# Windowed attention with a gated MLP on one core: a small value matmul placed later, and the hand-written opening closed off behind its last steps

## The chip, the cores and the metric

One core of a Trainium2 chip runs the whole program. The metric is device microseconds of one execution; the kernel before has three timed runs, and every comparison is made with their median. A profile is one more execution, recorded by the hardware profiler. TensorE is called PE here, its weight loads PEld; VectorE is DVE, ScalarE is ACT, GpSimd is POOL, and SyncE (SP) issues the DMAs.

## The reference

Eight batches of eight heads, 576 positions, head size 64. Each query sees itself and the 127 positions before it, with a bias that falls with distance. The heads, put side by side, are the rows x of a gated MLP whose gate mixes positions.

```python
scores = scale * q @ k.T                       # per batch and head, 576 x 576
scores = where((rel >= 0) & (rel < 128), scores - slope[h] * abs(rel), -1e9)
attn = exp(scores - max);  attn /= attn.sum() + 1e-9
x = concat_heads(attn @ v)                     # 8 x 576 x 512
h = gelu_tanh(x @ w_in);  u, v = split(h)      # 512 and 512 columns
v_n = (v - mean) / sqrt(var + 1e-6) * g_ln
v_s = w_sg @ v_n + b_sg                        # over positions
out = x + (u * v_s) @ w_out
```

## The kernel before

**The attention** goes by pairs of heads: 32 pairs, four to a batch, pair n belonging to batch n // 4. A pair is a row of one-letter steps (the table STEPS). `a` and `c` are the score matmuls (`*` is both in one burst: `a` into the two banks of the PSUM pool ps_a, `c` into the two of ps_s); `A`, `C` and `n` run on DVE and form bias, row minima and their copy nb; `E` is the exponentials on ACT (line 373), `R` the reciprocal of the sums on DVE, `r`, `s` and `S` the scaling on POOL (line 388). `t` and `T` are four PE transposes each (line 398) for the first and the second head, `X` and `Y` DVE's masked copies of them out of ps_a (px). The first 64 queries have a narrower window and go apart: `z` is one transpose for them (line 411), `P` ACT's copy of it into p0 (line 414), and `2` or `3` the value matmul of these queries, p0 against vd (line 418, with 64 columns; the profile counts two passes of it), into ps_a or into ps_s. `V` (or `v`, in ps_a) is the value matmul of all other queries (line 431, 36 short ones), `x` gathers both results into SBUF on ACT (lines 439 and 440), and `h`, `l`, `k` split the pair's rows into a high and a low part (lines 446, 451, 455) in one of four buffers xs. A buffer of xs comes free when all that a batch's MLP reads of it is done.

**The MLP** of a batch is a generator, `mlp_block`, which yields after each chunk of matmuls the columns that it streamed: `t` (the last 64 positions, line 532), the two v parts (two chunks each of 12 matmuls with 512 columns, lines 501 to 503), four u parts (two chunks each of 12 matmuls with 288 columns, lines 478 to 480), four mixing parts g (two chunks of 14, lines 570 to 574) and four output parts. Each v, u, g and output part takes one of the two buffers of the PSUM pool ps_m. A v part's buffer is given back by ACT's gelu into vg (line 523), and vg has one buffer only: the second v part's gelu follows the first one's normalization (DVE line 486 to 490, POOL's power at line 489, ACT line 491, DVE line 494). A u part's buffer is given back by ACT's copy at line 550.

**The order.** For PE everything is fixed by the order in which the program is written: each PE instruction is chained to the one before (`in_order`). For the other engines the first stretch is fixed, the list START at lines 604 to 611: each token is a step and a pair (`e3`), a stage of splitting a weight (`d`, `m`, `b`, `o`, `+`, `H`, `-`), a load (`i`), or one quarter of a v part of batch 0 (`w12`). It holds pairs 0 to 4 and the split of w_in, and its instructions are chained on each engine. After START the table PLAN at line 654 says at which share of a pair's time in MLP columns its steps are put between chunks; a step lands behind the chunk in which its time falls. There DVE, ACT, POOL and SP have no written order: the framework's scheduler orders them at build time, by its own clock, and may place instructions that are written later ahead of START's remaining ones on these engines. The splitting of w_sg and w_out (`decode`) is handed out along the DVE steps of the later pairs.

The order of PE around the steps of this change, in the batch with pairs 21 to 24 (chunks in small letters, a and b being the halves), was

```
*22  v2b  t21 z21  v0a  T21 3_21  v0b  V21  u0a u0b u1a  *23  u1b u2a  t22 z22  u2b
T22 3_22  u3a u3b g0a  V22  g0b g1a  *24  g1b g2a  t23 z23  g2b  T23 3_23  g3a g3b  V23
```

Of the kernel before, what the change touches and what calls it, by code (L numbers as in the profile page):

```python
# [21 lines left out]
def attention_gmlp(  # L22
# [17 lines left out]
    nc = tc.nc  # L40
# [464 lines left out]
    def mlp_block(b, xs, xfs):  # L505
# [85 lines left out]
    FIRST = 5  # L591
# [15 lines left out]
        z1 C2 s1 q4 S1 t1 X1 a3 P1 f2 o5 T1 +5 Y1 h0 R2 d4 21 v1 A3 s2 l0 x1 L3 H5 t2 m4 k0 w10 b4 e3 X2 -5 w20  # L607
        c3 o4 w00 r2 C3 +4 z2 w30 P2 h1 S2 f3 a4 l1 T2 Y2 w31 H4 R3 k1 22 v2 -4 d3 A4 w01 r3 L4 x2 s3 w11 h2 m3
        t3 S3 e4 z3 X3 w21 l2 c4 T3 b3 w02 o3 k2 w32 Y3 P3 +3 d6 w12 C4 23 v3 H3 i7 -3 w22 x3 m6 h3 b6 f4 l3 o6
        w13 k3 +6 R4 w23 d7 w03 r4 H6 w33 m7 s4 z4 P4 b7 t4 S4 X4 -6 T4 o7 Y4 +7 24 v4 H7 -7 x4 h4 l4 k4  # L610
    """
    started = {}
    last = {}
    wchunks = {}

    @contextmanager
    def in_order(engines=None):

        before = len(nc.cur_bb.bb.instructions)
        yield  # L620
        for i in nc.cur_bb.bb.instructions[before:]:
            if engines is None or i.engine in engines:
                if i.engine in last:
                    tc.add_manual_dep(i, last[i.engine], mybir.DependencyInfo(mybir.DependencyClass.NoSync, mybir.DependencyReason.DATA), reason="in_order")
                last[i.engine] = i.name
# [22 lines left out]
    FULL = (4 * 3 * NC * F + 2 * NC * F + 6 * NC * S2 * NF + 2 * (3 * T + 2) * S2 * NF + 6 * NF * S2 * NC) / NPAIR  # L648
    BEGINS = [0, 0.95, 1.7, 2.4, 3.0, 3.6, 4.4]

    def begin(n):
        return BEGINS[n - FIRST] * FULL if n - FIRST < len(BEGINS) else (BEGINS[-1] + n - FIRST - len(BEGINS) + 1) * FULL

    PLAN = [(0.0, "*ACnq"), (0.45, "ER"), (0.8, "rsS"), (1.25, "tzXP"), (1.4, "TY3"), (1.7, "VxhlkL")]
    events = []
    for n in range(FIRST, len(pairs)):
        for at, ops in PLAN:
            k = n + int(at)
            t = begin(k) + (at - int(at)) * (begin(k + 1) - begin(k))
            events.append((t, ops, n))  # L660
    events.sort(key=lambda x: x[0])

    nc.sync.dma_start(gb, g_ln.rearrange("(o f) -> o f", o=1).broadcast_to([P, F]))
    vec.steps = steps = decode()
    now = 0
    PE = [nc.tensor.engine]
    for n in (FIRST, FIRST + 1):
        Pair.STEPS["q"](pairs[n])
        if n == FIRST:
            Pair.STEPS["L"](pairs[n])  # L670
    with in_order(PE):
        while True:
# [14 lines left out]
                break  # L687
            now += cols
    assert not events


# [23 lines left out]
```

## Time and profile before

| | |
|---|---|
| timed runs, us | 717.34, 717.72 (median), 718.35 |
| the profiled execution, us | 715.63, with a span of 713.9 from its first to its last instruction |
| granted TensorE clock, mean | 0.958 of full speed |
| DMA | 56.28 MB in the kernel's own queue, 25.2% of 16 engines' span |

The profiled execution is 0.3% under the median of the timed runs. A row of the timeline gives start, duration (both in us from the span's start), engine, line, operation, result and operands, and in brackets the idle time of the engine ahead of it with what ended that. A row of the chain of waits gives the waiting engine and what it waited for: the total in us, the number of times, and the longest. A row of the table by windows gives, for a stretch of the span, its length, each engine's busy time, the granted clock (1.00 is full speed), the DMA share and GB/s.

### The profile page before, as it was taken

What the parts mean: (1) busy time and instruction counts of PE and PEld (TensorE: products, weight loads), DVE (VectorE), ACT (ScalarE), POOL (GpSimd) and SP (SyncE); (2) the same over time, 40 slices, a digit from 0 to 9 for tenths busy, and PEclk for the clock granted to TensorE, in tenths of its full rate; (3) what the DMA queues carried; (4) which work ended last, traced back from release to release, by engine and by line L of the source; (5) the groups of instructions that cost most, each with busy time, mean ns of one, the idle gap of its engine ahead of it and who ended that gap; (6) DMA issues with size and microseconds to landing.
All of it is one profiled execution on the core that took longest, in us unless ns stands there. A gap on an engine that the chain in (4) does not pass through costs nothing.

```text
span 713.9 us, 14846 instructions
## 1 busy us (share of the span) xinstructions
PE 625.7 (88%) x5664; PEld 563.9 (79%) x5664; DVE 416.8 (58%) x1372; ACT 357.1 (50%) x997; POOL 246.6 (35%) x243
## 2 busy tenths in 40 slices
PE   3795678789889979999799997999799997999997
PEld 2574667677789958898589976899589985899997
DVE  5885848666755567555666547555665555643512
ACT  7775367424664265534656346543655337530430
POOL 1687345532335203441224403351124412331220
PEclk9998899899999998999899999999999998999999
DMA  8646321134212422223122331224122220101001
GB/s 272 212 122 203 99 76 53 36 119 119 69 41 65 136 67 69 61 68 115 34 69 68 102 102 36 62 62 136 50 68 70 86 86 2 34 1 67 1 1 67
DMA packets 55931, 57.24 MB, mean 80 GB/s; under 512 B 8498, under 2 KB 45362, under 8 KB 55860
## 3 DMA queue, kind: packets, MB, share of 16 engines
q1 hardware_dynamic: 55860, 56.28, 25.2%
q8 instruction: 45, 0.74, 0.4%
q14 instruction: 26, 0.21, 0.1%
HBM read 46.83 MB, written 9.44 MB: 79 GB/s over the span
## 4 chain that ended last, share of the span: by engine, by line
PE 47%; DVE 22%; ACT 20%; POOL 4%; issue 4%; DMA 2%; SPq 1%; POOLq 0%; ACTq 0%; DVEq 0%
ACT e L373 10%; PE ps_m L478 7%; PE ps_m L479 6%; PE ps_m L480 6%; DVE e L266 6%; PE ps_s L431 5%; PE ps_m L570 3%; PE ps_m L571 3%; PE ps_m L572 3%; DVE st L486 2%; DVE vn L494 2%; ACT L373 2%; ACT L523 2%; PE ps_a L330 2%; POOL rs L489 2%
## 5 line engine op out<-in xcount | busy, mean ns | idle before, releaser
L373 ACT ACTIVATE e<-e,nb 128x128 f32<-128x128 f32 x270 | 101.9, 379 | 75.9 <-DVE nb L266 75.7
L388 POOL TENSOR_TENSOR e<-e,rr 128x512 f32<-128x512 f32 (+1 forms) x96 | 80.1, 857 | 140.3 <-DVE rr L266 71.3
L489 POOL TENSOR_TENSOR rs<-rs,mhalf 128x1 f32<-128x1 f32 (+1 forms) x40 | 35.9, 909 | 171.7 <-DVE rs L488 171.7
L570 PE MATMUL ps_m<-ws,vn 128*128 128x288 f32 x256 | 79.8, 312 | 0.0
L478 PE MATMUL ps_m<-xs,wi 128*128 128x288 f32 x256 | 78.1, 305 | 0.0
L478 PE MATMUL ps_m<-g,wo 128*128 128x288 f32 x256 | 78.0, 305 | 0.0
L479 PE MATMUL ps_m<-g,wo 128*128 128x288 f32 x256 | 76.2, 298 | 1.1 <-POOL g L257 1.1
L571 PE MATMUL ps_m<-ws,vn 128*128 128x288 f32 x256 | 76.8, 300 | 0.0
L572 PE MATMUL ps_m<-ws,vn 128*128 128x288 f32 x256 | 76.8, 300 | 0.0
L480 PE MATMUL ps_m<-g,wo 128*128 128x288 f32 x256 | 76.0, 297 | 0.0
L479 PE MATMUL ps_m<-xs,wi 128*128 128x288 f32 x256 | 75.7, 296 | 0.0
L480 PE MATMUL ps_m<-xs,wi 128*128 128x288 f32 x256 | 75.6, 295 | 0.0
L257 POOL TENSOR_TENSOR g<-u,g 128x576 fp32r<-128x576 f32 x32 | 45.5, 1422 | 78.9 <-ACT g L256 78.9
L501 PE MATMUL ps_m<-wi,xs 128*128 128x512 f32 x128 | 58.1, 454 | 3.8 <-ACT xs L446 3.8
L266 DVE TENSOR_TENSOR px<-ps_a,m_old 128x512 f32<-128x512 f32 x64 | 43.7, 682 | 27.5 <-PE ps_a L398 27.2
L503 PE MATMUL ps_m<-wi,xs 128*128 128x512 f32 x128 | 54.8, 428 | 1.3 <-POOL xs L451 1.3
L451 POOL TENSOR_TENSOR xs<-xf,xs 128x576 fp32r<-128x576 f32 x32 | 46.4, 1457 | 26.5 <-DVE xs L266 24.4
L502 PE MATMUL ps_m<-wi,xs 128*128 128x512 f32 x128 | 54.6, 426 | 0.0
L486 DVE BATCH_NORM_STATS2 st<-vg 128x6 f32<-128x512 f32 (+1 forms) x40 | 26.1, 685 | 45.9 <-ACT vg L523 38.1
L431 PEld LDWEIGHTS ps_s<-px,vt 128*64 128x64 f32 x972 | 47.0, 137 | 5.9 <-issue 5.3
L570 PEld LDWEIGHTS ps_m<-ws,vn 128*128 128x128 f32 x256 | 49.9, 195 | 2.1 <-issue 1.7
L256 ACT ACTIVATE g<-u 128x576 fp32r<-128x576 f32 x32 | 21.9, 683 | 59.5 <-DVE u L577 59.5
(125 smaller groups left out, 1617.7 us busy)
## 6 DMA issues: line engine op xcount, KB each, us to landing
qk<-qkT SPq DMA_DIRECT2D x32, 576.0 KB, 3.9
vt<-v_in SPq DMA_DIRECT2D x64, 256.0 KB, 3.3
outT<-xf SPq DMA_DIRECT2D x32, 288.0 KB, 2.1
wst<-w_in SPq DMA_DIRECT2D x8, 512.0 KB, 5.0
vt<-v_in SPq DMA_DIRECT2D x64, 32.0 KB, 2.9
wst<-w_out SPq DMA_DIRECT2D x4, 512.0 KB, 3.7
wst<-w_sgT SPq DMA_DIRECT2D x4, 288.0 KB, 4.3
vd<-v_in SPq DMA_DIRECT2D x64, 16.0 KB, 2.0
```

The lines of the kernel that those rows point to most:

```text
L266: inst = getattr(nc.vector, name)(*args, **kw)
L373: nc.scalar.activation(x, x, AF.Exp, bias=self.nm[0:n, i:i + 1], scale=-1.0, accum_out=self.sm[0:n, i:i + 1])
L388: nc.gpsimd.tensor_tensor(x, x, self.rr[0:n, i:i + m].rearrange("p (m o) -> p m o", o=1).broadcast_to([n, m, c]), ALU.mult)
L431: return lambda: nc.tensor.matmul(x1[heads[j], q0 + lo // 2 * R if t < 0 else q0 + t * R:q0 + (hi + 1) // 2 * R], block, px[j][:, (half * ...
L478: nc.tensor.matmul(dst, ah, bh, start=(i == 0), stop=False)
L479: nc.tensor.matmul(dst, ah, bl, start=False, stop=False)
L480: nc.tensor.matmul(dst, al, bh, start=False, stop=(i == n - 1))
L501: nc.tensor.matmul(pv[:, i, :], xh, wi[:, 0, c, F:], start=(c == 0), stop=False)
L503: nc.tensor.matmul(pv[:, i, :], xl, wi[:, 0, c, F:], start=False, stop=(c == NC - 1))
L570: nc.tensor.matmul(y, vn[:, 0, t, fs], ws[:, 0, t, ss], start=(t == 0), stop=False)
L571: nc.tensor.matmul(y, vn[:, 0, t, fs], ws[:, 1, t, ss], start=False, stop=False)
L572: nc.tensor.matmul(y, vn[:, 1, t, fs], ws[:, 0, t, ss], start=False, stop=False)
```

## The change

Three things are changed. The value matmul of the first queries (`3`) leaves its place right behind the second transposes (share 1.4 of a pair's time) for a place of its own at 1.6, one or two chunks of the MLP later, and the value matmul `V` with the gather and the split goes from 1.7 to 1.75, which for some pairs is one chunk later. The split of pair 4's rows (`h4 l4 k4`) leaves the end of START and becomes an entry of the plan, at 1.15 pair times. And all that is written after START on ACT, DVE, POOL and SP is ordered behind START's last instruction on the same engine; the order is one of issue, with no wait on a semaphore.

```diff
-        w13 k3 +6 R4 w23 d7 w03 r4 H6 w33 m7 s4 z4 P4 b7 t4 S4 X4 -6 T4 o7 Y4 +7 24 v4 H7 -7 x4 h4 l4 k4
+        w13 k3 +6 R4 w23 d7 w03 r4 H6 w33 m7 s4 z4 P4 b7 t4 S4 X4 -6 T4 o7 Y4 +7 24 v4 H7 -7 x4
...
-    PLAN = [(0.0, "*ACnq"), (0.45, "ER"), (0.8, "rsS"), (1.25, "tzXP"), (1.4, "TY3"), (1.7, "VxhlkL")]
+    PLAN = [(0.0, "*ACnq"), (0.45, "ER"), (0.8, "rsS"), (1.25, "tzXP"), (1.4, "TY"), (1.6, "3"), (1.75, "VxhlkL")]
...
+
+    events.append((1.15 * FULL, "hlk", FIRST - 1))
     events.sort(key=lambda x: x[0])
...
+    start_ends = dict(last)
+    first = len(nc.cur_bb.bb.instructions)
...
+    for i in nc.cur_bb.bb.instructions[first:]:
+        if i.engine in start_ends and i.engine not in PE:
+            tc.add_manual_dep(i, start_ends[i.engine], mybir.DependencyInfo(mybir.DependencyClass.NoSync, mybir.DependencyReason.DATA), reason="start")
```

With the new plan the order of PE in the same batch is

```
*22  v2b  t21 z21  v0a  T21  v0b 3_21  u0a  V21  u0b u1a  *23  u1b u2a  t22 z22  u2b
T22  u3a u3b 3_22  g0a  V22  g0b g1a  *24  g1b g2a  t23 z23  g2b  T23  g3a 3_23  g3b  V23
```

## The prediction

> **What bounds the kernel.** The page comes first, then the table of waits with PE as the waiting engine, over the whole span and then batch by batch (the last six rows are the windows 165.9 to 248.7, 248.7 to 331.5, 331.5 to 414.1, 414.1 to 496.7, 496.7 to 580 and 580 to 655.6).
>
> ```profile
> PE 625.7 (88%) x5664; PEld 563.9 (79%) x5664; DVE 416.8 (58%) x1372; ACT 357.1 (50%) x997; POOL 246.6 (35%) x243
> ...
> PE ps_s L418 <- ACT p L414: 35.4, 17, 5.0
> ...
> PE ps_s L418 <- ACT p L414: 2.9, 2, 2.6
> PE ps_s L418 <- ACT p L414: 6.3, 3, 5.0
> PE ps_s L418 <- ACT p L414: 6.6, 3, 5.0
> PE ps_s L418 <- ACT p L414: 6.9, 3, 5.0
> PE ps_s L418 <- ACT p L414: 6.3, 3, 5.0
> PE ps_s L418 <- ACT p L414: 6.0, 2, 5.0
> ```
>
> PE is the bound: 625.7 of 713.9 us busy. Of its 88 us of idle time 35.4 belong to one instruction, the matmul that the change moves, and 35.0 of those (2.9 + 6.3 + 6.6 + 6.9 + 6.3 + 6.0) to batches 1 to 6. So I read one of these batches, the one from 414.1, in the timeline; pair 21 stalls there for 5 us.
>
> ```profile
> 423.93 0.48 PE L501 MATMUL ps_m<-wi,xs 128*128 128x512 f32 x1
> 424.03 1.28 ACT L373 ACT_TABLE_LOAD   x1 [2.13 <-DVE nb L266]
> 426.81 0.60 PE L398 MATMUL ps_a<-ident,e 128*128 128x128 f32 x4
> 428.67 1.02 ACT L523 ACTIVATE vg<-ps_m 128x1024 f32<-128x1024 f32 x1
> 432.18 0.19 ACT L414 COPY p<-ps_a 128x64 f32<-128x64 f32 x1
> 432.42 0.69 PE L418 MATMUL ps_s<-p,vd 128*128 128x64 f32 x2 [5.01 <-ACT p L414]
> 437.06 1.88 PE L431 MATMUL ps_s<-px,vt 128*64 128x64 f32 x36
> 438.87 0.40 PE L478 MATMUL ps_m<-xs,wi 128*128 128x288 f32 x1
> 439.18 1.02 ACT L523 ACTIVATE vg<-ps_m 128x1024 f32<-128x1024 f32 x1
> 442.18 0.29 PE L478 MATMUL ps_m<-xs,wi 128*128 128x288 f32 x1
> ```
>
> PE ends T21 at 427.41 (426.81 + 0.60). ACT copies p0 only at 432.18, for in its queue that copy stands behind pair 22's exponentials, which start at 424.03 because their minima came late, and behind a gelu. PE's queue is in order, so a whole v chunk that is ready waits behind a matmul of 64 columns.
>
> **Part 1: the matmul moved.** ACT's queue does not depend on where PE puts `3`: the copy's chain runs from the minima (424.03) over ACT alone. So I keep the times of ACT, DVE and POOL as they are and walk PE through the new order. A v chunk is 2.88 us (423.93 to 426.81), `V` 1.81 (437.06 to 438.87), a u chunk 1.65 (438.87 to 442.18 is two). After T21 at 427.41 v0b ends at 430.3; `3` still waits for 432.42, 2.1 us instead of 5.0, and takes 0.45 (the next chunk starts at 432.87, where the first window below begins). u0a, V21 and u0b follow to 438.0. Then comes what is late next: u1a takes the PSUM buffer that the second gelu of the v parts gives back, at 440.20 (439.18 + 1.02). Before, u1a started at 442.18 and this was covered. So u1a starts at 440.20, with a new wait of 2.2 us: of the 5.0 only 2.0 is kept. ACT's gelu there hangs on the first part's normalization, again not on PE.
>
> ```profile
> 448.34 0.17 DVE L266 COPY nb<-stats 128x10 f32<-128x10 f32 x1
> 449.38 0.69 DVE L266 TENSOR_TENSOR px<-ps_a,m_old 128x512 f32<-128x512 f32 x1 [0.86 <-PE ps_a L398]
> 449.99 0.68 DVE L266 TENSOR_TENSOR px<-ps_a,m_own 128x512 f32<-128x512 f32 x1
> 450.90 0.60 PE L398 MATMUL ps_a<-ident,e 128*128 128x128 f32 x4
> 452.85 0.19 ACT L414 COPY p<-ps_a 128x64 f32<-128x64 f32 x1
> 452.94 0.63 ACT L550 COPY u<-ps_m 128x576 f32<-128x576 f32 x1
> 453.09 0.43 PE L418 MATMUL ps_s<-p,vd 128*128 128x64 f32 x2 [1.60 <-ACT p L414]
> 456.62 0.30 PE L570 MATMUL ps_m<-ws,vn 128*128 128x288 f32 x1
> ```
>
> PE comes to T22 at 448.9 (450.90 less 1.98), but it needs the bank that DVE's masked copies free. They waited 0.86 us for PE, so they can start at 448.52 and, lasting 1.29 (449.38 to 450.67), end at 449.8: a wait of 0.9 us. T22 ends at 450.4, u3a and u3b take 3.28 (453.34, where `3` ended, to 456.62) and end at 453.7; the copy of p0 (ending 453.04) is there, `3` takes 0.25, and g0a starts at 453.9, with u2's copy done at 453.57: 0.3 us of cover. That is 2.7 us before 456.62. Pair 23's wait, the rest of the 6.9 (0.28), goes as well: 3.0 us a batch, though 6.9 is removed. The same walk holds for the four batches from 248.7 to 580 (12.0) and, without pair 23's wait, for the next (2.7). In the batch from 165.9 the 2.9 us are all of the short kind, with nothing late behind them: 2.9. Sum 17.6, with the 0.3 left in batch 0 some 18 us. The other end, if ACT's and DVE's queues close up too, is the whole 35.0 and the slow clock behind the long stalls.
>
> ```profile
> 432.87:437.05 4.18, 4.18 (x14) 3.07 (x13) 3.83 (x7) 1.83 (x5) 4.18 (x5) 0.68 0.04 8
> 202.40:205.10 2.70, 0.09 (x2) 0.01 (x1) 1.41 (x3) 2.70 (x16) 0.00 (x0) 1.00 0.00 0
> 205.10:208.60 3.50, 3.50 (x26) 3.50 (x27) 1.25 (x4) 0.68 (x2) 2.64 (x4) 1.00 0.07 14
> 107.90:111.70 3.80, 1.21 (x9) 0.83 (x8) 3.55 (x18) 3.77 (x5) 1.81 (x2) 0.94 0.01 2
> 111.70:115.00 3.30, 3.30 (x15) 3.30 (x16) 1.50 (x6) 2.62 (x6) 2.37 (x2) 0.55 0.02 5
> ```
>
> After 5.0 us of waiting the v chunk takes 4.18 us at a clock of 0.68 instead of 2.88, 1.3 us lost, five times 6.5 (inside the walk's 3.0, outside the waits). After a wait of 2.6 us (202.40 to 205.10) the clock stays 1.00. So I take the new waits, 2.1, 2.2 and 0.9, as free of it.
>
> The plan's later `V` moves its loads of v, on SP's queue, one chunk at most; the buffers that they fill are read a pair's time later, so I cost them at nothing. `V`'s gather must free two ps_s banks before `*23`. From V21's end at 436.4 to the scores' second half it has about 5 us, and ACT's queue could hold it back by one or two copies: cost 0 to 2.5 us a batch; I take 0, as V's copy now stands directly behind the gelu. Pair 4's split stays where its buffer comes free, after u3 of batch 0: nothing.
>
> **Part 2: the opening.** Later work stands between START's steps now.
>
> ```profile
> 55.23 1.05 PE L431 MATMUL ps_a<-px,vt 128*64 128x128 f32 x19
> 58.54 0.68 ACT L256 ACTIVATE ws<-wst 128x576 fp32r<-128x576 f32 x1 [4.11 <-DMA wst<-w_sgT]
> 59.30 2.78 POOL L257 TENSOR_TENSOR ws<-wst,ws 128x576 fp32r<-128x576 f32 x2 [3.50 <-ACT ws L256]
> 65.77 5.51 DVE L241 TENSOR_SCALAR tmp<-tmp 128x512 f32<-128x512 f32 x1 [2.05 <-ACT tmp L239]
> 74.53 1.27 DVE L486 BATCH_NORM_STATS2 st<-vg 128x6 f32<-128x512 f32 x2
> 77.09 3.47 PE L431 MATMUL ps_a<-px,vt 128*64 128x64 f32 x36 [2.33 <-issue]
> 82.92 0.40 PE L478 MATMUL ps_m<-xs,wi 128*128 128x288 f32 x1
> ...
> PE ps_m L532 <- ACT u L550: 5.3, 1, 5.3
> ```
>
> The value matmul of pair 3 ends at 56.28 (55.23 + 1.05), yet ACT waits until 58.54 for a load of w_sg that only batch 0's mixing needs, with the gather of pair 3 behind it: 2.9 us. POOL's split of w_sg delays the next low part by some 1 us, and the statistics (1.27) stand ahead of the last masked copy: 5 us at least on the way to V4 at 77.09. The weight step of 5.51 us on DVE, which I take to be slowed by POOL's run beside it, may give back up to 4 more. But the held work comes after: ACT's four copies of w_sg, 0.68 each, and a gelu of 1.0 with a table load of 1.3, 5 us, now stand ahead of u0a at 82.92 (where the list's end frees ACT), and a second normalization of 8 us (428.67 to the gelu's table at 437.9, as in the walk's batch) between u0 and u1. Against that stands the 5.3 us that the t part waits behind u1's copy, which an earlier ACT can cut. Between 8 gained (nothing in the way after the list) and 3 lost (the list saves its 5, the lump costs 8), I take 3 gained, nearest to the row of 5.3. Waiting behind the list's last gather are all of ACT's later steps, so whatever delays V4 delays them all.
>
> [...]
>
> Sum: 18 + 3 = 21 us off the profiled execution's 715.63 gives 694.6. The median of the runs, 717.72, lies 0.3% above that execution, and on it the same saving gives **696.7**.
>
> **The rivals.** *All of the wait goes* (chance 0.10): the scheduler re-deals ACT's and DVE's queues so that the second gelu comes with the earlier PE. Then 35.0 + 6.5 + 3 = 44.5 us go, 673. Against it: the gelu at 439.18 hangs on ACT, DVE and POOL alone. *The wait is passed on* (0.13): the gather behind `V` is late, 2.5 of the 3.0 us are lost in five batches, and the opening gives nothing: 717.7 - 18 + 12.5 = 712. For it: an order on ACT that I cannot see. *It does not do what it says* (0.05): p0's copy moves back with its reader, and PE waits as before: 717.7. *The clock falls* (0.07), the slower side: one long wait becomes three short ones within 22 us, and PE's clock drops to half through that stretch. Place: v0b to T22, 430.3 to 450.4; price: its 15 us of matmuls, of which some 12 would double, stretch it by 12 less the 5.2 of waits, 6.8. It decides from 4.2 us a batch on, which is 3.0 and a fifth of the 5.9 saved elsewhere (2.9 + 3); at 6.8 the five batches lose 5 x 3.8 = 19: 717.7 + 19 - 5.9 = 731. For it: two waits at 107.9 to 111.7 with little between were followed by a clock of 0.55. Against it: 1.00 after 2.6 us.
>
> [...]
>
> **How the numbers follow.** My forecast has 0.65, with 685 to 705 as its own range (opening from 8 gained to 3 lost, the gather's cost). The range 679 to 713 leaves out most of the first rival and the last two, 0.2. A measurement of this kernel can tell about 0.2% (1.4 us) from no change. Faster: 0.65 + 0.10 + 0.13 = 0.88; same 0.05; slower 0.07.
>
> **What would show it.** The wait of L418 for L414 falls from 35.4 to about 11 (five times 2.1); new on PE's list are about 2.2 us ahead of a u part (L478) for ACT's gelu L523 and 0.9 us ahead of L398 for DVE's px, five times each; the batches shrink from 82.6 to 79.6; V4 comes before 72. Wrong would be: batches under 77 (the queues closed up), L418 still at 5.0, or clock under 0.9 over a batch.

## The result, and the profile after

Four runs of the changed kernel gave 691.40 to 695.67 us, median **694.61**, against 717.53 (716.23 to 718.35, four runs) of the kernel before on the same chip: a ratio of 0.9675, with a 95% interval of 0.9639 to 0.9710. The profiled execution took 695.0 us, its span is 693.3.

From the page of the changed kernel, PE's busy time, and from its table of waits the rows of PE:

```profile
PE 623.7 (90%) x5664; PEld 566.0 (82%) x5664; DVE 425.1 (61%) x1372; ACT 360.3 (52%) x999; POOL 246.4 (36%) x243
```

```profile
PE ps_s L418 <- ACT p L414: 11.1, 5, 2.2
...
PE ps_m L478 <- ACT u L550: 8.1, 2, 7.3
PE ps_m L478 <- ACT vg L523: 4.6, 3, 3.0
...
PE ps_a L398 <- ACT p L414: 3.3, 1, 3.3
```

PE worked as long as before within 2 us (623.7 against 625.7), so the gain is waiting that is gone. L418 waits 11.1 us in five times 2.2, as forecast, where it had 35.4. The two rows of L478 below it are new: the 7.3 us and one wait of 3.0 lie in the opening, the first sign that the two parts of the change pulled in opposite directions. The last row is a stall of batch 1.

To see where the time went I mark the start of the value matmul of pairs 3, 4, 5, 8, 12 and 28 (V3 to V28). Rows of PE's timeline, first of before (V4 stands in the prediction), then of after:

```profile
54.40 0.45 PE L431 MATMUL ps_a<-px,vt 128*64 128x64 f32 x6
...
117.60 0.66 PE L431 MATMUL ps_s<-px,vt 128*64 128x64 f32 x10
...
171.44 0.34 PE L431 MATMUL ps_s<-px,vt 128*64 128x64 f32 x4
...
246.91 0.45 PE L431 MATMUL ps_s<-px,vt 128*64 128x64 f32 x6
...
578.13 0.34 PE L431 MATMUL ps_s<-px,vt 128*64 128x64 f32 x4
```

```profile
59.80 0.45 PE L431 MATMUL ps_a<-px,vt 128*64 128x64 f32 x6
...
73.36 0.45 PE L431 MATMUL ps_a<-px,vt 128*64 128x64 f32 x5 [1.39 <-issue]
...
126.04 0.34 PE L431 MATMUL ps_s<-px,vt 128*64 128x64 f32 x4
...
177.19 0.34 PE L431 MATMUL ps_s<-px,vt 128*64 128x64 f32 x4
...
252.26 0.34 PE L431 MATMUL ps_s<-px,vt 128*64 128x64 f32 x4
...
562.06 0.34 PE L431 MATMUL ps_s<-px,vt 128*64 128x64 f32 x4
```

| stretch | before, us | after, us | difference | forecast |
|---|---|---|---|---|
| start to V3 | 54.40 | 59.80 | +5.4 | |
| V3 to V4 | 22.69 | 13.56 | -9.1 | |
| V4 to V5 | 40.51 | 52.68 | +12.2 | |
| V5 to V8 | 53.84 | 51.15 | -2.7 | -3.3 for all so far |
| V8 to V12 (batch 1) | 75.47 | 75.07 | -0.4 | -2.9 |
| V12 to V28 (batches 2 to 5) | 331.22 | 309.80 | -21.4 | -12.0 |
| V28 to the end of the span | 135.8 | 131.2 | -4.6 | -2.7 |
| whole span | 713.9 | 693.3 | -20.6 | -20.9 |

That the sum came out to the microsecond is luck, for its terms did not: the batches from V12 on gave 11.3 us more than forecast, the opening and batch 1 gave 11.5 us less. The 5.4 us ahead of V3 are a slow clock of this one execution (0.50 from 32.6 to 46.3 us; the opening is taken up behind the experiments); the rest needs reasons.

Next, one batch of each kernel, V20 to V24, from the table by windows: length, busy time of PE, PEld, DVE, ACT and POOL with their instructions, granted clock, DMA share, GB/s. Before, then after:

```profile
412.31:494.91 82.60, 75.72 (x710) 68.83 (x709) 48.82 (x167) 42.87 (x118) 26.02 (x25) 0.98 0.25 75
```

```profile
407.12:484.65 77.53, 75.31 (x710) 69.19 (x709) 50.66 (x168) 42.97 (x118) 25.92 (x25) 0.98 0.26 79
```

The batch lost 5.1 us, not 3.0. Length less PE's busy time is the waiting: 6.9 us before, 2.2 after, which is L418's one wait. The waits forecast ahead of u1a (2.2) and of T22 (0.9) are not in this batch at all. But the clock is 0.98 as before, which the forecast had left behind. The timeline of the same stretch, of PE, ACT, DVE and POOL:

```profile
418.04 0.40 PE L503 MATMUL ps_m<-wi,xs 128*128 128x512 f32 x1
418.85 1.28 ACT L373 ACT_TABLE_LOAD   x1 [2.13 <-DVE nb L266]
423.49 1.03 ACT L523 ACTIVATE vg<-ps_m 128x1024 f32<-128x1024 f32 x1
427.00 0.19 ACT L414 COPY p<-ps_a 128x64 f32<-128x64 f32 x1
427.24 0.43 PE L418 MATMUL ps_s<-p,vd 128*128 128x64 f32 x2 [2.22 <-ACT p L414]
429.08 0.75 DVE L494 SCALAR_TENSOR_TENSOR vn<-vg,rs,vn 128x512 fp32r<-128x512 f32 x1 [0.17 <-ACT vn L491]
429.17 2.92 POOL L388 TENSOR_TENSOR e<-e,rr 64x128 f32<-64x128 f32 x3
429.98 1.28 ACT L523 ACT_TABLE_LOAD   x1
429.99 2.65 DVE L494 SCALAR_TENSOR_TENSOR vn<-vg,rs,vn 128x512 fp32r<-128x512 f32 x1 [0.15 <-ACT vn L491]
432.67 1.02 ACT L523 ACTIVATE vg<-ps_m 128x1024 f32<-128x1024 f32 x1 [1.41 <-DVE vn L494]
```

Three things stand here. The second gelu's table load runs at 429.98 beside DVE's step and the gelu starts when that step ends; before, the load itself had waited for the step (2.75 us for vn, then 1.28 of load ahead of the gelu at 439.18). The chain to the second gelu is shorter by those 1.3 us (from V20 to this gelu 26.87 us before, 25.55 after), and u1a's wait with it. Second, the first gelu at 423.49 was ready at 418.44, when its chunk ended on PE: for 5 us it stands behind exponentials whose table load waits for their minima. Third, that late gelu splits the exponentials and keeps p0's copy until 427.00.

### The profile page after: what moved, and what is told of

Same layout as the page of the kernel before. It is cut to its first block, busy times and chain, and to the rows that moved or that the text cites. A ratio compares the mean times of both kernels' runs of the same rounds, so it can differ in the third digit from the quotient of the medians.

```text
span 693.3 us, 14860 instructions
## 1 busy us (share of the span) xinstructions
PE 623.7 (90%) x5664; PEld 566.0 (82%) x5664; DVE 425.1 (61%) x1372; ACT 360.3 (52%) x999; POOL 246.4 (36%) x243
## 4 chain that ended last, share of the span: by engine, by line
PE 62%; DVE 14%; ACT 11%; POOL 6%; issue 3%; DMA 3%; SPq 0%; POOLq 0%; ACTq 0%; DVEq 0%
PE ps_m L478 9%; PE ps_m L479 8%; PE ps_m L480 8%; PE ps_s L431 6%; PE ps_m L570 5%; PE ps_m L572 4%; PE ps_m L571 4%; ACT e L373 3%; PE ps_a L398 3%; DVE e L266 3%; PE ps_s L330 2%; PE ps_a L330 2%; ACT L373 2%; POOL e L388 2%; DMA wst<-w_in 2%
## 5 line engine op out<-in xcount | busy, mean ns | idle before, releaser
L478 PE MATMUL ps_m<-xs,wi 128*128 128x288 f32 x256 | 81.5, 318 | 12.8 <-ACT u L550 8.1
L570 PE MATMUL ps_m<-ws,vn 128*128 128x288 f32 x256 | 81.0, 316 | 0.0
L478 PE MATMUL ps_m<-g,wo 128*128 128x288 f32 x256 | 77.9, 304 | 0.0
L479 PE MATMUL ps_m<-xs,wi 128*128 128x288 f32 x256 | 77.9, 304 | 0.0
L480 PE MATMUL ps_m<-xs,wi 128*128 128x288 f32 x256 | 77.8, 304 | 0.0
L479 PE MATMUL ps_m<-g,wo 128*128 128x288 f32 x256 | 76.4, 298 | 1.0 <-POOL g L257 1.0
L478 PEld LDWEIGHTS ps_m<-xs,wi 128*128 128x128 f32 x256 | 50.3, 196 | 16.7 <-ACT u L550 8.8
L501 PE MATMUL ps_m<-wi,xs 128*128 128x512 f32 x128 | 54.6, 427 | 0.6 <-ACT xs L446 0.6
L486 DVE BATCH_NORM_STATS2 st<-vg 128x6 f32<-128x512 f32 (+1 forms) x40 | 26.1, 685 | 46.3 <-ACT vg L523 38.5
L398 PE MATMUL ps_a<-ident,e 128*128 128x128 f32 x256 | 42.3, 291 | 13.1 <-POOL tmp L248 4.4
L330 PE MATMUL ps_s<-qk 64*64 64x192 f32 (+2 forms) x632 | 42.2, 359 | 13.0 <-DMA qk<-qkT 8.2
L503 PE MATMUL ps_m<-wi,xs 128*128 128x512 f32 x128 | 52.0, 406 | 0.8 <-POOL xs L451 0.8
L502 PE MATMUL ps_m<-wi,xs 128*128 128x512 f32 x128 | 52.0, 406 | 0.0
```

The lines of the kernel that those rows point to most:

```text
L330: return lambda: nc.tensor.matmul(dst, qk[js, 0, q0:q0 + R], qk[js, 1, k0:k1], start=True, stop=True)
L398: burst([lambda t=t: nc.tensor.transpose(ct[:, t * P:(t + 1) * P], self.pr[j][:, t, :], ident) for t in range(T)])
L478: nc.tensor.matmul(dst, ah, bh, start=(i == 0), stop=False)
L479: nc.tensor.matmul(dst, ah, bl, start=False, stop=False)
L480: nc.tensor.matmul(dst, al, bh, start=False, stop=(i == n - 1))
L501: nc.tensor.matmul(pv[:, i, :], xh, wi[:, 0, c, F:], start=(c == 0), stop=False)
```

## The experiments

All times are medians of a kernel's runs, with the ratio to the kernel before on the same chip and its 95% interval (beside the experiments that kernel took 716.65 to 717.92 us); "batch" is V20 to V24 in the profiled execution. Line numbers of kernels with added lines are up to 8 higher (L422 is L414 of before, L531 is L523, L558 is L550, L578 is L570, L487 is L479).

| kernel | us | ratio | batch, us |
|---|---|---|---|
| the change | 694.61 | 0.9675 [0.9639, 0.9710] | 77.53 |
| move_only | 687.94 | 0.9590 [0.9563, 0.9617] | 77.53 |
| hold_only | 719.04 | 1.0013 [0.9992, 1.0035] | 82.61 |
| x2_behind | 696.97 | 0.9724 [0.9678, 0.9770] | 78.73 |
| three_at_V | 695.22 | 0.9709 [0.9672, 0.9746] | 78.33 |
| p_first | 674.97 | 0.9402 [0.9345, 0.9460] | 75.03 |
| move_p_first | 677.87 | 0.9436 [0.9379, 0.9493] | 74.98 |
| move_vg2 | 717.42 | 0.9982 [0.9950, 1.0015] | 83.63 |
| move_vg2_p | 700.93 | 0.9768 [0.9717, 0.9819] | 79.59 |
| gelu_first | 694.86 | 0.9690 [0.9651, 0.9729] | 77.07 |
| after_gelu_first | 670.67 | 0.9353 [0.9329, 0.9378] | 73.47 |
| hold_split | 691.06 | 0.9631 [0.9604, 0.9657] | 77.41 |
| split_gelu_first | 671.36 | 0.9355 [0.9326, 0.9385] | 73.47 |

### The two halves: move_only, hold_only

move_only is the kernel before with the changed PLAN alone; hold_only has the shorter START and the order behind it, with the old PLAN.

```diff
-    PLAN = [(0.0, "*ACnq"), (0.45, "ER"), (0.8, "rsS"), (1.25, "tzXP"), (1.4, "TY3"), (1.7, "VxhlkL")]
+    PLAN = [(0.0, "*ACnq"), (0.45, "ER"), (0.8, "rsS"), (1.25, "tzXP"), (1.4, "TY"), (1.6, "3"), (1.75, "VxhlkL")]
```

Expected of move_only: 

> The matmul and V moved by the new plan; the opening list and the free order behind it as before. My theory now: the move is all of the gain and the hold is about neutral. Then the wait of L418 for L414 is 11 us (five of 2.2), the batches from the third on take 77.5 us as with the whole change, and the time is 692 to 697. The rival, that the hold in the opening saves some 3 us as I predicted: 697 to 700. A second rival, that the hold costs what the changed kernel lags in its opening (8 us at pair 5's value matmul): 685 to 689.

Expected of hold_only: 

> The hold and the shorter list, with the matmul and V at their old places. My theory now: neutral, 716 to 719, L418 waits about 35 us as before, batches 82.6 us. The predicted gain of the opening: 713 to 715. The rival that the hold costs 5 to 8 us: 722 to 726. The lag of 5.4 us at pair 3's value matmul, where both kernels still run the same instructions on PE, DVE, ACT and POOL, I put down to PE's clock being at half from 32.6 to 46.3 us in that one execution; then it need not be in this one, and if the hold makes it, it is.

The move alone takes 687.94 us, 6.7 less than the whole change and inside the second rival's range, with the same batches of 77.53. The hold alone leaves the time as it was. Its V4 and V5 in PE's timeline:

```profile
68.55 0.41 PE L431 MATMUL ps_a<-px,vt 128*64 128x64 f32 x5 [1.39 <-issue]
...
117.79 0.34 PE L431 MATMUL ps_s<-px,vt 128*64 128x64 f32 x4
```

V4 is 8.5 us earlier than before, V5 0.2 later (117.60 before): all that the closed opening gains is given back at once. So the gain is the move's alone, and beside the move the hold costs.

### Why the batch fell by 5.1 and not by 3.0: x2_behind, three_at_V

ACT's small gather (L440, which reads what `3` wrote) runs between the first gelu and the second, before as after. But in the changed kernel `3` stands behind v0b on PE, so that by the build's order that copy takes over the wait on PE for v0b; the gelu is left with the one for DVE, and its table load has none. x2_behind is the change with that copy put behind the large gather, so that the gelu has both waits again:

```diff
-            nc.scalar.copy(xf[:, R:S].rearrange("p (t h c) -> p h t c", t=T, h=2), self.x1.rearrange("p (h t c) -> p h t c", t=T, h=2))
-            nc.scalar.copy(xf[:, 0:R], self.x2[:, 0:R])
+            big = nc.scalar.copy(xf[:, R:S].rearrange("p (t h c) -> p h t c", t=T, h=2), self.x1.rearrange("p (h t c) -> p h t c", t=T, h=2))
+            with tc.issue_after(big.ins):
+                nc.scalar.copy(xf[:, 0:R], self.x2[:, 0:R])
```

Expected: 

> The whole change, with ACT's small gather copy (L440) queued behind the large one (L439). PE's order is the same. My theory: in the changed kernel the second v gelu's table load runs early, since the small copy has already waited for PE behind v0b and the gelu needs DVE alone, so that the wait no longer stands on the table load; this hides 1.3 us on the chain that bounds the batch. With the copy behind, the wait comes back to the table load: it starts after DVE's vn, the gelu ends 1.3 us later from T21's end, the batches take 78.8 to 79.6 us, the time 700 to 705. The rival, that the shorter batch comes from PE's order alone: 77.5 us and 693 to 697.

ACT's timeline of x2_behind:

```profile
428.37 1.28 ACT L524 ACT_TABLE_LOAD   x1 [2.76 <-DVE vn L495]
429.66 1.02 ACT L524 ACTIVATE vg<-ps_m 128x1024 f32<-128x1024 f32 x1
```

The load waits for DVE again and stands ahead of the gelu, and the batch is 78.73 us, 1.2 longer: the size of a load (1.28). From V20 to the second gelu it is 26.87 us again, as before. So the load is 1.3 of the 2.2 us that are missing at u1a. The rest is PE's own lateness: with the load back, x2_behind waits there for 0.6 us and not 2.2, in each of the four batches from V12 to V28, and each of them has the slow clock behind `3` (0.98 over the batch). The expected run time was too high by some 3 us, probably as it set out from a median whose executions differ in their opening; batches of profiled executions are the better measure here.

three_at_V is the change with `3` still later, together with `V` ((1.4, "TY"), (1.75, "3VxhlkL") in PLAN).

Expected: 

> The whole change, with the small matmul one more chunk later, directly ahead of V. My theory: the batch is bound by the chain over ACT's gelus, not by what is left of the wait. L418's wait falls from 2.2 to under 0.7 us a batch, PE waits 1.5 to 3 us ahead of u1a for the gelu instead, the batches take 76.5 to 77.5 us, the time 691 to 695. The rival, that the 2.2 us and the slow clock behind it (1.8 us) are all to be had: 73.5 us a batch and 675 to 680.

From its table of waits of PE:

```profile
PE ps_m L478 <- ACT vg L523: 15.3, 6, 3.0
```

L418 now waits 3.1 us in all, and PE waits for the second gelu instead, 12.3 us in the five batches (15.3 less the opening's 3.0). The batch is 78.33, 0.8 longer than the change's and above the 77.5 that I had set as the most. So two paths meet ahead of u1a, PE's own and the gelu's, and taking the wait off the first shows the second.

### What holds both paths: p_first, move_p_first, gelu_first

The rows of the batch named one suspect for both: the next pair's exponentials, which ACT's queue has ahead of the first gelu and of p0's copy. p_first is the kernel before, `3` in its old place, with the exponentials issued behind the copy of p0 (the first gelu comes ahead of that copy by itself); move_p_first adds the move.

```diff
+        def exps_behind(self):
+            prev = getattr(pairs[self.n - 1], "copied", None) if self.n > FIRST else None
+            if prev is None:
+                self.exps(range(T))
+            else:
+                with tc.issue_after(prev.ins):
+                    self.exps(range(T))
...
-            "n": copy_minima, "E": lambda p: p.exps(range(T)), "e": lambda p: p.exps(range(0, 2)), "f": lambda p: p.exps(range(2, T), False),
+            "n": copy_minima, "E": lambda p: p.exps_behind(), "e": lambda p: p.exps(range(0, 2)), "f": lambda p: p.exps(range(2, T), False),
...
-            nc.scalar.copy(self.p0, self.ct0[:, 0:R])
+            self.copied = nc.scalar.copy(self.p0, self.ct0[:, 0:R])
```

Expected of p_first: 

> The kernel before (the matmul stays ahead of v0b), with one edit on ACT's queue: the next pair's exponentials go behind the copy of p0 instead of ahead of it. Theory (two paths of about the same length meet ahead of u1a: PE's own list, and the gelus with their normalizations, which hang on ACT's small gather copy and on the table load): the 35.4 us of L418 behind L414 all but vanish, yet part of it comes back ahead of a u part for the gelu of the v parts; batches of 80 to 82 us instead of 82.6, the run 705 to 714. Rival: ACT's place for the copy is all that matters; the wait and the slow clock behind it go, batches of 75 to 76 us, the run near 676.

Expected of move_p_first: 

> The matmul's move alone, with the next pair's exponentials behind the copy of p0 on ACT. The five waits of 2.2 us at L418 go. Theory (two paths meet ahead of u1a): PE then waits for the gelu instead, batches stay at 77 to 78 us, the run 685 to 690. Rival (what is left is PE's path alone): 2.2 of wait and 1.8 of slow clock go, batches of 73.5 us, the run 668 to 672.

My theory fell in both; in p_first the rival came in, in move_p_first the batch of 74.98 lies between the two. ACT's timeline of p_first, and its batch:

```profile
409.14 1.03 ACT L531 ACTIVATE vg<-ps_m 128x1024 f32<-128x1024 f32 x1 [1.80 <-PE ps_m L511]
410.07 0.21 ACT L422 COPY p<-ps_a 128x64 f32<-128x64 f32 x1
...
419.05 1.03 ACT L531 ACTIVATE vg<-ps_m 128x1024 f32<-128x1024 f32 x1
```

```profile
397.74:472.77 75.03, 74.18 (x710) 67.70 (x709) 49.51 (x167) 39.94 (x116) 25.62 (x26) 1.00 0.27 82
```

The first gelu waits for PE alone, p0's copy follows it, and the exponentials come in one piece. PE waits 0.85 us in the batch at full clock, where before it waited 6.9 at 0.98. One edit on ACT's queue, with PE's order untouched, gives more (674.97) than the move (687.94), and with it the move adds nothing (batches of 75.03 and 74.98). I had put the two paths down to two causes; they have one, the place of the exponentials.

gelu_first asks which of the two instructions it is: the exponentials go behind the first gelu only, and p0's copy stays behind five of them.

```diff
+            if self.n < FIRST + 2 or not gelus:
+                self.exps(range(T))
+            else:
+                with tc.issue_after(gelus[-1].ins):
+                    self.exps(range(T))
...
-            nc.scalar.activation(vg, pv, AF.Gelu_apprx_tanh)
+            gelus.append(nc.scalar.activation(vg, pv, AF.Gelu_apprx_tanh))
```

Expected: 

> The kernel before (the matmul ahead of the v chunk, no hold), with one edit on ACT's queue: the next pair's exponentials go behind the gelu of the v part's first half, which is ready before their minima are. The copy of p0 stays behind five of them. Theory (the late first gelu is the cause of all of it: it makes the copy of p0 late, splits the exponentials with two more table loads, and pushes the normalization's last step on DVE into POOL's run): the gelu comes 5 us earlier, L418 waits at most 0.6 us instead of 5.0, batches of 75 to 76 us, the run 673 to 680, as with the copy first. Rival (the copy's place is what counted): L418 still waits 2 us or more in five batches, batches of 77 us or more, the run 686 or more.

Its wait at `3`, and its batch:

```profile
PE ps_s L426 <- ACT p L422: 18.0, 17, 2.6
```

```profile
411.01:488.08 77.07, 74.30 (x710) 67.72 (x709) 46.80 (x167) 39.88 (x116) 25.61 (x25) 1.00 0.26 80
```

Here the rival is right. The gelu is early, no wait for it is left and the clock is full, but p0's copy still keeps PE: 2.8 us a batch, 77.07. The late gelu accounts for 5.5 us of a batch (82.60 to 77.07), not for all of it: in the four batches from V12 to V28 the wait for p0's copy falls from 26.1 to 11.0 us. The run of 694.86 us is longer than move_only's though its batch is shorter. In its profile V3 comes at 59.10 us, where before has 54.40 (the slow clock of the opening again), and V8 to V12 take 80.40 us against 75.47 before, at a clock of 0.96; why that batch grew I have not traced.

### Making room in vg: move_vg2, move_vg2_p

With a second vg buffer the second gelu need not wait for the first normalization. To fit it, one x buffer of eight went, and a small tile shared a tag.

```diff
-            xf = self.xf = mlp.tile([P, S], F32, name="xf", bufs=2 * NC)
+            xf = self.xf = mlp.tile([P, S], F32, name="xf", bufs=2 * NC - 1)
...
-            vg = mlp.tile([P, 2, F], F32, name="vg", bufs=1)
+            vg = mlp.tile([P, 2, F], F32, name="vg", bufs=2)
```

Expected of move_vg2: 

> The matmul's move alone, with a second vg buffer, so that the second gelu need not wait for the first normalization's last reader (room for it: one x buffer less, and one small tile shares a tag). Theory (two paths meet ahead of u1a): the gelus come up to 5 us earlier, but PE still waits 2.2 us for the copy of p0 and runs slow behind it; batches of 76.5 to 78 us, the run 683 to 688. Rival (the gelu chain alone sets the end): 3 to 4 us a batch less, batches of 73.5 to 74.5 us, the run 669 to 674.

Expected of move_vg2_p: 

> The matmul's move with both edits, the exponentials behind the copy of p0 and the second vg buffer. Theory (two paths that end together ahead of u1a): now both are short, neither the wait of 2.2 us nor the slow clock of 1.8 us behind it is left; batches of 73 to 74.5 us, the run 667 to 673. Rival (something else, the normalization's work on DVE and POOL, sets the rate of the batches): as the better of the two alone, 683 to 688, batches of 76.5 us or more.

PE's waits in the four batches from V12 to V28 of move_vg2:

```profile
PE ps_s L330 <- ACT xf L439: 11.4, 4, 3.1
```

This wait is new. The gather waits for an x buffer, and the next scores for the gather, 2.8 to 3.1 us a batch. Both runs missed both of their forecasts (717.42 and 700.93 us), and as the lost x buffer is mixed with the second vg buffer they settle nothing on the gelus.

### The hold: hold_split, after_gelu_first, split_gelu_first

hold_split is the change with only the steps of the weight splitting held behind START; after_gelu_first is the whole change with gelu_first's edit; split_gelu_first has hold_split's and gelu_first's.

```diff
-    for i in nc.cur_bb.bb.instructions[first:]:
+    for i in split_steps:
         if i.engine in start_ends and i.engine not in PE:
```

Expected of hold_split: 

> The whole change, but only the splitting of the weights is held behind the opening list; gelus, normalizations and gathers are free to go between its steps as before. Theory (what the whole hold gives back is the lump behind it: the first gelu and its normalization late, and u0's copy behind them): value matmul of pair 4 at 69 to 73 us, the wait of 7.4 us for u0's copy under 5, value matmul of pair 5 no later than with the move alone (117.5), the run 682 to 688. Rival (the split itself, in one lump behind the list, is the price): pair 5 at 120 us or later, the run 692 to 696 as with the whole hold.

Expected of after_gelu_first: 

> The whole change with the exponentials behind the first gelu. Theory (the hold costs 4 to 7 us between the value matmuls of pairs 4 and 5 and saves nothing that lasts; the moved matmul is worth nothing once the gelu is early): batches of 75 to 76 us, the run 676 to 684, 3 to 7 us above the kernel before with the same edit. Rival (the hold's price is only there where the batches have slack): the same time as that kernel within 2 us.

Expected of split_gelu_first: 

> The move, the hold of the weight splitting alone, and the exponentials behind the first gelu. Theory (each is free of the others): batches of 75 to 76 us, the opening of the kernel with the split held, the run 666 to 675 if that hold gains its 0 to 6 us, the fastest of all. Rival (the split in one lump is the price of the hold): as the whole change with the same edit, 676 to 684.

after_gelu_first has the lowest median, 670.67 us (670.33 to 671.77), faster than both kernels. split_gelu_first, 671.36 us (668.77 to 677.33) and inside its theory's range, can't be told from it, and has the same batch; so with an early gelu the runs don't tell the whole hold from that of the split alone. Its neighbour without any hold, the move with the early gelu, was not run. The timeline of after_gelu_first on ACT and DVE, and its batch:

```profile
406.42 1.03 ACT L531 ACTIVATE vg<-ps_m 128x1024 f32<-128x1024 f32 x1 [1.81 <-PE ps_m L511]
410.71 0.19 ACT L422 COPY p<-ps_a 128x64 f32<-128x64 f32 x1
414.17 0.69 DVE L502 SCALAR_TENSOR_TENSOR vn<-vg,rs,vn 128x512 fp32r<-128x512 f32 x1
415.37 1.03 ACT L531 ACTIVATE vg<-ps_m 128x1024 f32<-128x1024 f32 x1
```

```profile
395.02:468.49 73.47, 73.47 (x709) 67.81 (x708) 48.78 (x168) 39.99 (x116) 25.61 (x25) 1.00 0.28 84
```

PE is busy for all of 73.47 us. I had expected the moved matmul to be worth nothing once the gelu is early; it is worth 3.6 us a batch (77.07 to 73.47), since the copy of p0 at 410.71 is in time for a `3` that stands behind a chunk, and late for one that doesn't. The move takes 5.1 us off a batch, the early gelu 5.5, both together 9.1, a little less than their sum.

What the hold costs is less plain. Here is what lies behind V4 in the changed kernel, on ACT and PE:

```profile
77.28 2.41 ACT L256 ACTIVATE ws<-wst 128x576 fp32r<-128x576 f32 x4
81.00 1.02 ACT L523 ACTIVATE vg<-ps_m 128x1024 f32<-128x1024 f32 x1
...
82.08 0.40 PE L478 MATMUL ps_m<-xs,wi 128*128 128x288 f32 x1 [3.00 <-ACT vg L523]
...
92.21 0.62 ACT L550 COPY u<-ps_m 128x576 f32<-128x576 f32 x1
...
92.88 0.61 PE L478 MATMUL ps_m<-xs,wi 128*128 128x288 f32 x1 [7.35 <-ACT u L550]
```

The four copies of w_sg and the gelu come ahead of u0, 3.0 us of waiting; u0's copy, for which PE has waited since 85.53, stands in ACT's queue behind the rest of the lump and seven exponentials, 7.35 us. hold_split took the gelu out of the lump, and its wait for u0's copy fell only to 5.8; its V5 is 2.7 us nearer to V3 than with the move alone (60.04 against 62.73 us), but by V12 that is gone (190.28 against 189.63), and its 691.06 us lie between the move alone and the whole change. From V3 to V12 the whole change takes 192.46 us, 2.8 more than the move alone; hold_only takes 192.08 there and before 192.51, so that beside the old plan the hold costs nothing.

The other part of the 6.7 us between move_only and the change is not settled. In the profiled execution of the change PE ran at half clock for 13.7 us in the opening, in that of move_only it did not, with the same instructions up to there on PE, ACT, DVE and POOL (rows of the table by windows, after, then move_only):

```profile
32.60:46.30 13.70, 11.77 (x88) 9.71 (x92) 8.88 (x31) 6.64 (x27) 6.65 (x7) 0.50 0.31 92
```

```profile
32.60:46.30 13.70, 11.22 (x132) 8.57 (x130) 11.41 (x43) 10.02 (x40) 10.40 (x9) 1.00 0.45 134
```

It put V3 back by some 5 us in six of the fourteen profiled executions, three of the seven with a hold and three of the seven without (p_first and gelu_first among them). In the six, the window of the clock's grid ahead of the drop (the last section has this grid) held 1.4 to 2.1 us of idle PE (2.1 in the change, from 29.2 to 32.6); in the other eight no window between 24 and 45 us held more than 1.53 (1.37 in before); the two ranges overlap a little. That it goes by where the grid falls in an execution is my reading of these ranges, and no run tests it. Whether the hold makes it more frequent the runs don't tell.

## Why the prediction came true, and where its steps were wrong

The forecast of 696.7 us lies 2.1 above 694.61, and the direction was right for the reason given: PE stood in its queue behind 64 columns, and moving them lets a v chunk through. L418's wait is the forecast's, five times 2.2. The rest is a sum of errors that cancel, 11.3 us on one side and 11.5 on the other, and that they cancel so well is luck.

- **The wait ahead of u1a (2.2 us a batch forecast; 0 or 0.8 measured).** The failed step is "I keep the times of ACT, DVE and POOL as they are". Up to p0's copy they held; then the wait on PE moved from the second gelu to the small copy ahead of it, and the gelu's table load lost its wait: 1.3 us, shown by x2_behind. The 0.9 us forecast ahead of T22 measured 0.2 or nothing. The load is not the cause of that, for x2_behind has 0.2 there as well; from the second gelu's end to the masked copies DVE takes 7.8 us in both, where it took 8.3 before with a gap of 0.40 us for ACT's vn, and the rest is not traced. The danger that I did weigh, the first rival, was of this kind, and I gave it the whole wait or nothing.
- **The clock (the new waits taken "as free of it").** Wrong: behind three of the five waits of 2.2 us PE ran at half clock for 3.4 us (0.50 from 350.07, 428.58 and 582.18), those of which 2.08 to 2.22 us fell into one window of the clock's grid; behind the other two, split over two windows, it stayed at 1.00. In the batch V20 to V24 u0a and V21 behind it take 5.14 us (427.49 to 432.63) where the walk has 3.46, 1.7 us lost. It did no more harm because the gelu's path is as long: the two batches without the drop wait 0.8 us for the gelu instead, and take 77.4 us too.
- **Batch 1 (2.9 forecast, 0.4 measured).** The wait at L418 went, but the next wait for p0's copy, ahead of a transpose, grew from 2.6 to 3.3 us, and the clock fell behind it (0.51 from 189.6 to 196.5 us, after a window with 2.4 of 3.4 us idle), which the walk didn't follow.
- **The opening and batch 0 (3.3 saved forecast).** Up to V8 5.75 us were lost, 5.4 of them to the slow clock of the profiled execution and 0.35 beside it. "V4 before 72" was right but for that clock (73.36 with it; 68.0 to 68.6 in four kernels with the same list that ran without it). The gain of 8.5 to 9.1 us at V4 was even the forecast's upper end; the failed step is the size of what is given back. The lump of ACT's work cost 3.0 and 7.35 us of PE's waiting where I had put 8 against 5, and nothing was left of the term of 3 (from V3 to V8 the change loses 0.35 us, hold_only gains 0.45). The weight step that took 5.51 us beside POOL's run takes 0.40 at 66.10 in the changed kernel, where POOL is beside it for 0.17 (0.41 to 0.43 in both kernels where POOL is idle). Beside POOL's scaling DVE's second vn step takes 2.65 us in the batch shown; the first, which starts 0.09 us ahead of that run, takes 0.75. Such a meeting is not what ate the opening's gain: there POOL's four subtractions run from 78.05 to 83.57 us, and the one long normalization step that starts beside them, the statistics at 82.06, takes 1.29 us, as before (1.27); the step at 84.61, beside POOL's next split, takes 1.16 us where it took 0.74.
- **The rivals.** "The clock falls" named the right mechanism at the wrong size: a drop to 0.50 for 3.4 us behind one wait, not through the whole stretch, and the clock over a batch stays at 0.98. "All of the wait goes" was near the truth of what can be had: after_gelu_first's batch saves 9.1 us, five times of which with the rest gives 670.67 against my 673. It needed a change on ACT's queue.

What I missed altogether is the row that I quoted: the first gelu at 428.67 in the prediction's timeline, with a table load of exponentials ahead of it that waited for minima. I read it as a given. It was the cause of the larger part of the wait that the change works around, as gelu_first shows (26.1 us of it fall to 11.0); the five exponentials ahead of the copy are the rest.

## What to carry to other kernels

When PE waits for a small copy on another engine, look at what stands ahead of that copy in its queue, and since when it has been ready: reordering the late engine gave 42 us here (p_first) where moving the waiting matmul gave 30 (move_only). The two gains add only as far as each takes away a wait that the other leaves: beside p_first the move is worth nothing, beside the early gelu 3.6 us a batch. Before a walk keeps another engine's times, ask which semaphore wait goes over to an earlier instruction: here a table load that lost its wait was hidden, 1.28 us. Closing off an opening moves the held work into one lump; price the lump by the first instruction behind it for which the bound engine waits.

## What the runs showed of the hardware

**PE's clock changed on a grid of 3.41 us, and fell behind windows in which PE idled for about 2 us or more.** In the profiles of before and after the clock's changes lie on a grid of 3.41 us: in after it falls to 0.50 at 350.07, is back at 1.00 at 353.48, and falls again 22 such steps later, at 428.58. The table by windows of the changed kernel, two waits of 2.2 us:

```profile
346.70:350.10 3.40, 1.18 (x7) 0.68 (x5) 2.99 (x8) 3.37 (x12) 0.25 (x1) 1.00 0.00 0
350.10:353.50 3.40, 3.40 (x20) 3.12 (x20) 3.06 (x7) 2.84 (x6) 3.40 (x4) 0.50 0.06 14
500.30:503.70 3.40, 2.25 (x10) 1.50 (x8) 1.62 (x4) 3.36 (x5) 0.00 (x0) 1.00 0.00 0
503.70:507.10 3.40, 2.33 (x22) 2.17 (x24) 3.21 (x10) 2.86 (x14) 2.28 (x3) 1.00 0.02 5
507.10:510.50 3.40, 3.35 (x46) 3.06 (x40) 2.91 (x2) 1.97 (x3) 2.51 (x3) 1.00 0.11 31
```

The first wait lies whole in one window, 2.2 of 3.4 us idle, and the next window has half the clock (0.50). The second is split, 1.15 and 1.07 us, and the clock stays at 1.00. In before and after, from where their records of the clock begin (29.3 and 25.8 us) and counting windows whose successor ends within the span, 44 at full clock had at least 0.85 us of idle PE: 19 were followed by half clock, with 2.02 to 3.41 us idle, and 25 were not, with at most 1.71. Over the fourteen profiles the border is less sharp. From 140 us on 123 windows at full clock had at least 0.85 us of idle PE: 54 were followed by half clock, with 1.91 to 3.41 us idle but for one of 1.65; 69 were not, with at most 1.70 us but for one of 1.93. Ahead of 140 us seven drops follow windows with 1.37 to 1.70 us idle, and windows with up to 1.85 us pass. The 2.6 us of before from which I took the clock as safe were split too, with 1.1 us ahead of 203.4 and 1.7 behind:

```profile
200.00:203.40 3.40, 2.29 (x17) 1.85 (x15) 2.55 (x9) 2.85 (x13) 0.00 (x0) 1.00 0.00 0
203.40:206.80 3.40, 1.71 (x13) 1.71 (x14) 0.80 (x3) 2.38 (x13) 1.23 (x2) 1.00 0.02 5
206.80:210.20 3.40, 3.40 (x28) 3.40 (x28) 1.27 (x3) 1.37 (x2) 3.00 (x4) 1.00 0.05 10
```

**The same table load was hidden or bare by which of two waits its gelu kept.** The 1.28 us of L523's load stand behind the wait for DVE in before and x2_behind, and beside it in the changed kernel, with the same instructions in all three.
